# Even slots' middle maxima ahead of their ends, and the 128-column scores ahead of the 384, in a windowed attention with a gated MLP

## The chip, the cores and the metric

One core of one Trainium2 chip runs the whole program. The metric is the device time of one execution in microseconds (us). Engines are named as in the profile: PE (matmul), PEld (its weight loads, which run beside the matmuls), DVE (vector), ACT (scalar), POOL (GpSimd), SP (the queue that issues the transfers).

## The reference

```python
B, S, D = 1, 2048, 512           # H = 32 heads of 16, window W = 256, F = 1792
xn = layernorm(x)
q, k, v = split(xn @ wqkv)
scores = q @ k.T * 16 ** -0.5     # per head; key j is seen by query i where 0 <= i - j < 256
s = (softmax(masked scores) @ v) @ wo
g = silu(gelu(layernorm(xn) @ w1 + b1) @ w2 + b2)
return x + s * g
```

All is float32. The kernel gets products of float32 precision by splitting operands into a high and a low part (two or three matmuls for one).

## The kernel before, in words

The program has three stretches. Up to about 59 us it loads `x`, normalizes it and makes the first projections. From 59 to 391 us it does the attention, with the other projections, and the first of the MLP's matmuls, filled in between. After that come the rest of the MLP, the output projection and the gate. The change touches the second stretch alone.

The attention's work is cut into eight groups of four heads, and each group into 16 slots, one for a block of 128 tokens. One pass of the loop over `u` is a slot pair, called a pair here: an even slot and an odd one, 64 pairs in all. Every instruction goes out in the order in which the code writes it, on each engine (a wrapper keeps the program's order, so nearly all rows of the profile have that wrapper's line, L42, and are told apart by their tiles). On an engine an instruction that waits holds up all that stands behind it.

The tiles in PSUM (eight banks) that matter here:

- `stb`, two banks: scores of a pair, in three parts one after the other. PE fills it, ACT's exponential reads it into a tile `pt`, and only then can PE fill it again. Parts 0 and 1 are two heads each: the first key block against up to 384 queries, and the second key block against its own 128 queries. Part 2 holds the second key block's other 256 queries for all four heads; the last pair of a group has none.
- `xy`, two banks: the *ends* of a row's maximum. For a query block 12 slots ahead (`LEAD`), PE computes the scores with the own key block and the block two before; DVE merges them by the mask (COPY_PREDICATED) and reduces to a maximum, kept in `mt`.
- `zo`, two banks, shared. Columns 0 to 255 of both banks are `mids`, the *middle* of a row's maximum: scores with the key block one before, which DVE reduces into `mt` too. Columns 256 to 511 of the second bank are `otb`, in which PE sums the products of the exponentials with the values (`pv_part`, in the profile `zo<-pt,vt`). ACT copies `otb` to SBUF as `oraw` when a pair's products are done.
- `fb`, two banks: the fills, matmuls of projections or of the MLP, of 512 columns mostly, two at a time in the two halves of the array's rows. A table gives each slot its fills, and `some(parts[...])` issues them.

A score or maximum matmul uses 64 rows of the array, so that those for `a` = 1 and 0 run beside each other.

In a pair PE's order before is: scores part 1, ends, some fills, middle, fills (even slot); scores part 2, fills, middle, fills, ends, fills, scores of the next pair's part 0, and the value products (odd slot). ACT's order is: exponential of part 0, copy `oraw` (of the products just made), exponential of part 1, exponential of part 2, with copies and casts for the projections between. For a group's first block (seven times behind the first pair) there is no middle.

Of the kernel before, what the change touches and what calls it, by code (L numbers as in the profile page):

```python
# [25 lines left out]
LEAD = 12  # L26
# [23 lines left out]
def mixer_kernel(ctx, tc, x, wqk, wv, wo, w1, b1, w2, b2, out):  # L50
# [97 lines left out]
    def run(steps):  # L148
        for step in steps:
            step()  # L150
# [471 lines left out]
    def prob_part(u, part):  # L622

        n, kb = u // 8, 2 * (u % 8)
        if part == 2 and kb == 14:
            return
        slot = slots[n % 2]
        both = stb[0]
        if 16 * n + kb + LEAD >= 16 * NQ and (3 * u + (part + 3) % 3) % 2:
            both = xy  # L630
        pt = pp.tile([P, 2, 512], F32, tag="pt", name=f"pt_{u}_{part}")

        def scores(at_, a, p, k, q, w):
            r = slice(64 * a, 64 * a + 64)
            nc.tensor.matmul(both[:, a, at_: at_ + w], slot[r, 1, p, P * k: P * (k + 1)],
                             slot[r, 0, p, P * q: P * q + w], start=True, stop=True)
        if part < 2:
            w = min(384, S - P * kb)
            for a in (1, 0):
                scores(128, a, part, kb, kb, w)  # L640
            for a in (1, 0):
                scores(0, a, part, kb + 1, kb + 1, 128)
            w += 128
        else:
            w = 512
            for p in range(2):
                for a in (1, 0):
                    scores(256 * p, a, p, kb + 1, kb + 2, 256)
        outs["exp"] = nc.scalar.activation(pt[:, :, 0:w], both[:, :, 0:w], AF.Exp, scale=DH ** -0.5)

        def select(at_, step, pattern, compare, by):
            nc.gpsimd.affine_select(out=at_, in_=at_, pattern=pattern, compare_op=compare, fill=0.0, base=0,
                                    channel_multiplier=by)
        if part < 2:
            own = pt[:, :, 0:256].rearrange("k a (b q) -> k a b q", b=2)
            select(own, 1, [[0, 2], [0, 2], [1, P]], ALU.is_ge, -1)
            if w == 512:
                select(pt[:, :, 384:512], 1, [[0, 2], [-1, P]], ALU.is_gt, 1)
        else:
            last = pt.rearrange("k a (p q) -> k a p q", p=2)[:, :, :, 128:256]  # L660
            select(last, 1, [[0, 2], [0, 2], [-1, P]], ALU.is_gt, 1)
        pts[u, part] = pt

    def pv_part(u):

        n, kb = u // 8, 2 * (u % 8)
        seq = [(kb, lambda j: pts[u, j // 2][:, j % 2, 128:384], 0, 256),
               (kb + 1, lambda j: pts[u, j // 2][:, j % 2, 0:128], 128, 256)]
        if kb:
            seq[:0] = [(kb - 1, lambda j: pts[u - 1, 2][:, j % 2, 256 * (j // 2): 256 * (j // 2 + 1)], 0, 256),  # L670
                       (kb - 2, lambda j: pts[u - 1, j // 2][:, j % 2, 384:512], 0, 128)]
        for i, (k, of, lo, hi) in enumerate(seq):
            for j in range(4):
                nc.tensor.matmul(otb[32 * j: 32 * j + DH + 1, lo: hi], vt[:, k, (4 * n + j) % 16], of(j),
                                 start=(i == 0), stop=(i == len(seq) - 1),
                                 skip_group_check=True, tile_position=(0, 32 * j))
        oraw = sgp.tile([P, 256], F32, tag="or", name=f"oraw_{u}", bufs=2)
        nc.scalar.copy(oraw, otb)
        cols = slice(P * kb, P * (kb + 2))
        at(2 * u + 2, nc.sync.dma_start, oT_d[n, :, :, cols].rearrange("j r t -> (j r) t"), oraw)  # L680
# [256 lines left out]
    def fill_in(t, half):  # L937
        now[:] = t, half
        run(delayed.pop((t, half), ()))
        for fn, args in fills.get((t, half), ()):  # L940
            fn(*args)

    def planned(t):
        for fn, args in plan.get(t, []):
            fn(*args)

    def ended(t):
        for fn, args in ends.get(t, []):
            fn(*args)
# [3 lines left out]
    def own_max(part, m):  # L953
        return part(m // 16, m % 16) if m < end else lambda: None

    def own_rows(m, t):
        if 0 <= m < end and m % 4 == 3:
            max_rows(m // 16, m % 16 // 4, t)

    for t in range(-16, 0):  # L960
        m = t + LEAD
        if t == -5:
            open_slot(1)
            for k in range(4):
                at(-4 + k // 2 * 2, clear_part, k)
        fill_in(t, 0)
        planned(t)
        if 4 <= m < LEAD:
            max_block(0, m)
        fill_in(t, 1)  # L970
        if t == -1:
            early.close()
            stb.append(attn.enter_context(tc.tile_pool(name="ps_s2", bufs=1, space=PSUM)).tile(
                [P, 2, 512], F32, name="stb"))
            prob_part(0, 0)
            fill_in(t, 2)
        if 0 <= m < 4:
            max_block(0, m)
        run(lns.get(t, ()))
        own_rows(m, t)  # L980
        ended(t)
    def parted(todo, *cuts):

        n = sum(fn.__name__ == "unit" for fn, _ in todo)
        at_ = [0, *(-(-n * k // 20) for k in cuts), len(todo)]
        return [todo[a: b] for a, b in zip(at_, at_[1:])]

    def some(todo):
        for fn, args in todo:
            fn(*args)  # L990
    for u in range(end // 2):
        t = 2 * u
        prob_part(u, 1)
        rest = own_max(max_ends, t + LEAD)
        calm[0] = t < end - LEAD
        even, odd = (fills.pop((v, 0), []) for v in (t, t + 1))
        if u % 8:
            parts = parted(even, 5) + parted(odd, 10 if u % 8 == 7 else 5, 15)
        else:
            parts = parted(even + odd, 2, 6, 10, 14)  # L1000
        now[:] = t, 0
        run(delayed.pop((t, 0), ()))
        some(parts[0])
        own_max(max_middle, t + LEAD)
        rest()
        planned(t)
        some(parts[1])
        fill_in(t, 1)
        ended(t)
        t += 1  # L1010
        prob_part(u, 2)
        now[:] = t, 0
        run(delayed.pop((t, 0), ()))
        some(parts[2])
        own_max(max_middle, t + LEAD)
        some(parts[3])
        planned(t)
        fill_in(t, 1)
        own_max(max_ends, t + LEAD)()
        calm[0] = False  # L1020
        own_rows(t + LEAD, t)
        for fn, args in todo_dve:
            fn(*args)
        todo_dve.clear()
        if u % 8:
            some(parts[4])
        if t + 1 < end:
            prob_part(u + 1, 0)
        if u % 8 == 0:
            some(parts[4])  # L1030
        fill_in(t, 2)
        pv_part(u)
        ended(t)
# [29 lines left out]
    for f in range(6, NF, 2):  # L1063
        t = gp.tile([P, 2, 512], F32, tag="ohl", name=f"hr_{f}", bufs=4)
# [200 lines left out]
    for c in range(2):  # L1265
# [30 lines left out]
        for i in range(NF + 1):  # L1296
# [29 lines left out]
            k = i - o_from  # L1326
# [190 lines left out]
```

## Time and profile before

| what | value |
|---|---|
| median of three runs | 712.68 us (711.99 to 713.08) |
| the profiled execution | 711.56 us, its span 709.5 us |
| granted PE clock | 1.00 |
| PE busy | 702.7 us (99%), weight loads 571.9 us (81%) |
| DVE busy | 508.6 us (72%) |
| ACT busy | 407.5 us (57%) |
| POOL busy | 299.3 us (42%) |

The span runs from the first to the last instruction of the profiled execution. A matmul's time in a row includes its way through the array, and, where it waited for its weights, that wait; so the busy share of PE alone doesn't say how full it is, and starts of rows that follow each other say more. A row of the timeline has start, length, engine, line, operation, out<-in, and in brackets how long the engine was idle before it and on what.

### The profile page before, as it was taken

To read this page: it belongs to the slowest core of one execution; us is meant where nothing else is said; L and a number is where in the kernel's file an instruction comes from. 1 tells how busy PE (TensorE), PEld (TensorE's weight loads), DVE (VectorE), ACT (ScalarE), POOL (GpSimd) and SP (SyncE) were. 2 spreads that over 40 slices of the span, in tenths; PEclk is the share of its full clock that TensorE was granted. 3 is DMA by queue.
4 is the path that set the end of the run, shared out by engine and by line. 5 is a ranking of instruction groups with operands and counts; after the bars stand their busy time and mean duration, and the time that the engine had idled before them with its cause. 6 is when DMAs were issued, how large, how long until landed. Compare 5 with 4: busy or idle time off the path is not lost.

```text
span 709.5 us, 17676 instructions
## 1 busy us (share of the span) xinstructions
PE 702.7 (99%) x6912; PEld 571.9 (81%) x6912; DVE 508.6 (72%) x863; ACT 407.5 (57%) x604; POOL 299.3 (42%) x496
## 2 busy tenths in 40 slices
PE   8999999999999999999999999999999999999997
PEld 8999777777778887777777788888888888888886
DVE  7887787887877678788875666347686766766923
ACT  8767777778676667778877554222355545531001
POOL 7344766766676555767877420204203000002002
PEclk9999999999999999999999999999999999999999
DMA  8325466775549967678543747354222312353701
GB/s 307 80 49 123 93 147 156 186 177 133 117 118 272 296 221 231 166 192 206 173 137 114 264 141 264 104 157 154 90 90 89 120 59 90 99 184 125 232 15 60
DMA packets 66274, 106.95 MB, mean 151 GB/s; under 512 B 12624, under 2 KB 21072, under 8 KB 66192
## 3 DMA queue, kind: packets, MB, share of 16 engines
q1 hardware_dynamic: 66192, 105.82, 51.6%
q8 instruction: 55, 0.90, 0.5%
q14 instruction: 27, 0.22, 0.1%
HBM read 54.80 MB, written 33.82 MB: 125 GB/s over the span
## 4 chain that ended last, share of the span: by engine, by line
PE 98%; DMA 1%; DVE 0%; ACT 0%; issue 0%; POOL 0%; SPq 0%; DVEq 0%
PE fb L42 22%; PE acc L42 21%; PE zo L42 15%; PE p L42 9%; PE stb L42 8%; PE s L42 6%; PE h L42 6%; PE xy L42 6%; PE pv L42 2%; DMA x<-in_x_dram 1%; PE tr L42 0%; PE pair_-8_609 L42 0%; PE pair_-5_829 L42 0%; PE pair_-8_608 L42 0%; PE pair_-3_975 L42 0%; PE pair_-3_974 L42 0%
## 5 line engine op out<-in xcount | busy, mean ns | idle before, releaser
L42 ACT ACTIVATE pt<-stb 128x1024 f32<-128x1024 f32 (+1 forms) x176 | 177.6, 1009 | 51.6 <-PE stb L42 44.4
L42 POOL TENSOR_SCALAR_AFFINE_SELECT pt<-pt 128x512 f32<-128x512 f32 (+1 forms) x296 | 163.8, 574 | 72.9 <-ACT pt L42 69.9
L42 PE MATMUL fb<-xnT,wqb 64*128 64x512 f32 (+2 forms) x732 | 118.1, 392 | 0.2
L42 DVE COPY_PREDICATED xy<-upper,xy 128x512 f32<-128x512 int32 x128 | 88.9, 694 | 37.8 <-PE xy L42 35.2
L42 POOL TENSOR_TENSOR xo<-xo,gated 128x512 f32<-128x512 f32 x15 | 20.0, 1330 | 221.7 <-DVE gated L42 220.6
L42 PE MATMUL acc<-w,gh 128*128 128x512 f32 x320 | 98.6, 389 | 0.0
L42 PE MATMUL zo<-pt,vt 128*17 128x128 f32 (+1 forms) x1920 | 90.5, 327 | 0.3
L42 DVE TENSOR_REDUCE mt<-xy 128x4 f32<-128x512 f32 x128 | 88.0, 687 | 2.3
L42 DVE TENSOR_REDUCE mt<-zo 128x4 f32<-128x512 f32 x120 | 82.6, 689 | 6.3 <-PE zo L42 5.8
L42 PE MATMUL stb<-qk 64*128 64x384 f32 (+1 forms) x704 | 77.4, 297 | 0.0
L42 PEld LDWEIGHTS zo<-pt,vt 128*17 128x17 f32 x1920 | 49.1, 97 | 33.6 <-issue 1.3
L42 PEld LDWEIGHTS stb<-qk 64*128 64x128 f32 x704 | 55.4, 185 | 22.8 <-ACT pt L42 13.6
L42 PEld LDWEIGHTS acc<-w,gh 128*128 128x128 f32 x320 | 60.1, 188 | 12.5
L42 PEld LDWEIGHTS fb<-xnT,wqb 64*128 64x128 f32 (+1 forms) x732 | 61.3, 186 | 3.7 <-PE fb L42 1.0
L42 PE MATMUL acc<-w,gl 128*128 128x512 f32 x160 | 62.2, 389 | 0.0
L42 PE MATMUL xy<-qk 64*128 64x256 f32 (+2 forms) x576 | 60.3, 291 | 0.0
L42 PEld LDWEIGHTS xy<-qk 64*128 64x128 f32 x576 | 46.5, 185 | 7.3 <-DVE mt L42 1.2
L42 PE MATMUL p<-xnT 128*128 128x512 f32 x189 | 51.8, 389 | 0.0
L42 PEld LDWEIGHTS zo<-qk 64*128 64x128 f32 x480 | 40.5, 185 | 6.4 <-DVE mt L42 1.7
L42 PE MATMUL s<-wos,ohl 128*128 128x512 f32 (+1 forms) x204 | 44.3, 376 | 0.0
L42 ACT ACTIVATE gated<-acc 128x512 f32<-128x512 f32 x16 | 8.7, 596 | 62.0 <-DVE acc L42 62.0
L42 PE MATMUL fb<-xnT 64*128 64x512 f32 (+1 forms) x240 | 43.7, 403 | 0.5 <-DVE pjr L42 0.5
(205 smaller groups left out, 1214.4 us busy)
## 6 DMA issues: line engine op xcount, KB each, us to landing
qk<-sh SPq DMA_DIRECT2D x128, 128.0 KB
qk<-pjr SPq DMA_DIRECT2D x64, 128.0 KB
oT_d<-oraw SPq DMA_DIRECT2D x64, 128.0 KB
w_d<-in_w_dram SPq DMA_DIRECT2D x14, 512.0 KB
xt_d<-xnT SPq DMA_DIRECT2D x12, 512.0 KB
x<-in_x_dram SPq DMA_DIRECT2D x16, 256.0 KB
w<-w_d SPq DMA_DIRECT2D x16, 256.0 KB
or<-oT_d SPq DMA_DIRECT2D x16, 256.0 KB
```

The lines of the kernel that those rows point to most:

```text
L42: r = issue(*args, **kwargs)
```

## The change

Two things change, both in the attention's pairs. In `prob_part`, part 1's two matmuls of 128 columns come before its two of 384 (part 0 keeps its order). In the loop over `u`, the even slot's middle maxima come directly behind the scores of part 1, and the ends, with DVE's merge and reduction, behind the first fills. The odd slot is as it was.

```diff
         if part < 2:
             w = min(384, S - P * kb)
-            for a in (1, 0):
-                scores(128, a, part, kb, kb, w)
-            for a in (1, 0):
-                scores(0, a, part, kb + 1, kb + 1, 128)
+            for at_, k, wide in ((0, kb + 1, 128), (128, kb, w))[::1 if part else -1]:
+                for a in (1, 0):
+                    scores(at_, a, part, k, k, wide)
             w += 128
...
         prob_part(u, 1)
-        rest = own_max(max_ends, t + LEAD)
+        own_max(max_middle, t + LEAD)
         calm[0] = t < end - LEAD
...
         some(parts[0])
-        own_max(max_middle, t + LEAD)
-        rest()
+        own_max(max_ends, t + LEAD)()
         planned(t)
```

On PE, in an even slot (the pair at 165.7 us), from the scores of part 1 (`stb`) to those of part 2. `xy` are the ends, `zo` from `qk` the middle, `fb` the fills; in brackets stand the engines and transfer queues whose work is waited for. Before:

```order
L42 MATMUL stb<-qk_94 128x384 [waits Activation_49]
L42 MATMUL stb<-qk_94 128x384
L42 MATMUL stb<-qk_94 128x128 x2
L42 MATMUL xy<-qk_764 128x256 [waits DMAHW4_49,DMAHW3_49,DMAHW5_49,DMAHW1_49,DMAHW7_49,DMAHW0_49,DVE_49]
L42 MATMUL xy<-qk_764 128x256 x3
L42 MATMUL fb_112<-xnT,wqb_2503 128x512
L42 MATMUL fb_111<-xnT,wqb_2503 128x512
L42 MATMUL zo<-qk_764 128x128 [waits Activation_49]
L42 MATMUL zo<-qk_764 128x128 x3
L42 MATMUL fb_112<-xnT,wqb_2503 128x512
```

The same place on PE after the change:

```order
L42 MATMUL stb<-qk_94 128x128 [waits Activation_49]
L42 MATMUL stb<-qk_94 128x128
L42 MATMUL stb<-qk_94 128x384 x2
L42 MATMUL zo<-qk_764 128x128 [waits DMAHW5_49,DMAHW3_49,DMAHW7_49,DMAHW1_49,Activation_49]
L42 MATMUL zo<-qk_764 128x128 x3
L42 MATMUL fb_112<-xnT,wqb_2503 128x512
L42 MATMUL fb_111<-xnT,wqb_2503 128x512
L42 MATMUL xy<-qk_764 128x256 [waits DMAHW4_49,DMAHW0_49,DVE_49]
L42 MATMUL xy<-qk_764 128x256 x3
L42 MATMUL fb_112<-xnT,wqb_2503 128x512
```

The middle moved ahead of the ends and of one pair of fills, with its wait for ACT. By the program's counts that wait is for the copy `oraw` of the pair before, which before stood behind the ends and a fill on PE.

ACT's order is the same before and after; here are its rows around the copy for which the next pair's middle waits, with the exponentials (`pt_0`, `pt_1`, `pt_2` are the parts):

```order
L42 ACTIVATE pt_0_3058<-stb 128x1024 [waits PE_49]
L42 COPY oraw_3082<-zo 128x256 [waits DVE_49,DMAHW6_49,PE_49,Activation_49]
L42 ACTIVATE pt_1_3085<-stb 128x1024 [waits PE_49,Pool_49]
L42 ACTIVATE pt_2_3113<-stb 128x1024 [waits PE_49]
L42 COPY pjr_2_3146<-fb_111 128x512 [waits DMAHW1_49,PE_49]
```

Nothing moved on ACT: the copy stands between the exponentials of parts 0 and 1, and waits for PE's products, for DVE, and for the store of an earlier `oraw`.

On DVE, in the same pair, before (`mt` from `zo` is the middle's reduction, `mt` from `xy` that of the ends):

```order
L42 COPY_PREDICATED xy<-upper,xy 128x4x128 [waits PE_49]
L42 TENSOR_REDUCE mt_4_3001<-zo 128x4 [waits PE_49,Activation_49]
L42 TENSOR_REDUCE mt_4_3001<-xy 128x4 [waits DVE_49]
L42 TENSOR_REDUCE mt_4_3001<-zo 128x4 [waits PE_49]
L42 COPY_PREDICATED xy<-upper,xy 128x4x128 [waits DVE_49,PE_49]
```

And after:

```order
L42 TENSOR_REDUCE mt_4_3001<-zo 128x4 [waits PE_49,Activation_49]
L42 COPY_PREDICATED xy<-upper,xy 128x4x128 [waits PE_49]
L42 TENSOR_REDUCE mt_4_3001<-xy 128x4 [waits DVE_49]
L42 TENSOR_REDUCE mt_4_3001<-zo 128x4 [waits PE_49]
L42 COPY_PREDICATED xy<-upper,xy 128x4x128 [waits DVE_49,PE_49]
```

The middle's reduction moved from behind the ends' merge to ahead of it; the odd slot's two behind them stay. POOL's and SP's orders are the same.

## The prediction

> **What bounds the kernel now.** I read the engines' busy shares first, then the row of the attention stretch, then the chain of work there, then the waits, and last the timeline of single slot pairs ("pairs" below; one is a pass of the loop over `u`).
>
> ```profile
> span 709.5 us, 17676 instructions
> 59.00:391.00 332.00, 331.01 (x4868) 258.22 (x4866) 261.28 (x440) 248.31 (x336) 226.26 (x409) 1.00 0.64 172
> by line: PE fb L42 41.0%; PE zo L42 31.6%; PE stb L42 16.5%; PE xy L42 10.4%; DVE pjr L42 0.2%; issue 0.2%; DVE vt L42 0.1%; PE pair_-3_974 L42 0.0%; DVEq L42 0.0%; PE pair_-3_975 L42 0.0%
> PEld stb L42 <- ACT pt L42: 13.6, 63, 0.4
> PEld stb L42 <- issue: 6.5, 31, 0.2
> PEld zo L42 <- DVE mt L42: 1.7, 6, 0.4
> PEld xy L42 <- DVE mt L42: 1.0, 5, 0.2
> ACT oraw L42 <- PE zo L42: 19.3, 41, 0.9
> ```
>
> The second row is the stretch that the change touches, 59 to 391 us: PE busy 331.01 of 332.00 us, DVE 261, ACT 248, clock 1.00. The third is the chain in that stretch: four groups of matmuls hold 99.5% of it. So PE sets the time, and a stall put into its queue comes out at the end unless PE was going to stand there anyway. The waits are small: PE's weight loads for the scores (`stb`) wait 13.6 us for ACT's exponentials and 6.5 us after the value products, some 0.2 us a time, and 2.7 us for DVE's reductions.
>
> **What moves, and the wait that comes with it.** The kinds and numbers of instructions stay, no transfer is moved, and ACT's, POOL's and SP's orders stay. In an even slot PE's four middle-maxima matmuls (128 columns, into `mids`, half of `zo`) now stand right behind the scores; the four of the ends come one fill later. The middle ones wait for ACT, and by the program's counts for one instruction: the copy `oraw<-zo` of the pair before, which empties the other half of a bank that `mids` has a part in. Once in this trace that wait shows by itself:
>
> ```profile
> 108.99 0.37 ACT L42 COPY oraw<-zo 128x256 f32<-128x256 f32 x1 [0.86 <-PE zo L42]
> 109.41 0.30 PEld L42 LDWEIGHTS zo<-qk 64*128 64x128 f32 x4 [0.18 <-ACT oraw L42]
>   PEld zo L42: 0.2, 1
> ```
>
> The copy ends at 109.36 and the weights start at 109.41, 0.05 later. The last row (from the view of that copy, under who waited for it) says that this was felt once, for 0.2 us. In all other pairs the ends and a fill cover it. So the rows say that the wait is live. The Trainium skill (PSUM — Partial Sum Buffer, Terms) speaks against the change at the same place: two engines may not be in one bank and quadrant at once, so the middle maxima could not be let past the copy though their columns differ. If banks could be shared at will, the wait would be worth nothing and the sum below would be a gain of about 1 us; by the rule it is what follows.
>
> **How long PE stands.** Before, the ends' weights go in right behind the scores' matmuls; that row's start is the place the middle maxima take. The copy's end plus 0.05, less that start, is the new stall.
>
> ```profile
> 66.99 0.38 ACT L42 COPY oraw<-zo 128x256 f32<-128x256 f32 x1
> 67.13 0.30 PEld L42 LDWEIGHTS xy<-qk 64*128 64x128 f32 x4
> ...
> 160.51 0.30 PEld L42 LDWEIGHTS stb<-qk 64*128 64x128 f32 x4 [0.22 <-ACT pt L42]
> 160.79 0.30 PEld L42 LDWEIGHTS xy<-qk 64*128 64x128 f32 x4
> 160.81 0.40 ACT L42 COPY oraw<-zo 128x256 f32<-128x256 f32 x1
> ...
> 165.83 0.37 ACT L42 COPY oraw<-zo 128x256 f32<-128x256 f32 x1 [0.43 <-PE zo L42]
> 165.98 0.30 PEld L42 LDWEIGHTS xy<-qk 64*128 64x128 f32 x4
> ...
> 363.71 0.37 ACT L42 COPY oraw<-zo 128x256 f32<-128x256 f32 x1 [0.56 <-PE zo L42]
> 363.81 0.30 PEld L42 LDWEIGHTS xy<-qk 64*128 64x128 f32 x4
> ```
>
> First pair: 66.99 + 0.38 + 0.05 - 67.13 = 0.29. Pair at 165.8: 0.27. Last pair: 0.32. There ACT was free and waited for the value products (41 times in the stretch, by the waits). Where ACT was still at an exponential or a copy, as at 160.81, it is 160.81 + 0.40 + 0.05 - 160.79 = 0.47. Of the 57 pairs behind the first, seven have no middle maxima (a head group's first block). The other 50 run from the first pair above to the last; going through them, 37 are of the first kind (0.25 to 0.38, mean 0.32) and 13 of the second (twelve near 0.47, one 0.60, mean 0.48). 37 x 0.32 + 13 x 0.48 = 18.0 us.
>
> Behind the waiting load on PE stand the fill, the ends, the later fills and the second half's scores; DVE waits for the middle maxima and the ends, ACT for the next scores, POOL for ACT.
>
> **What PE gets back.** Where PE already stood ahead of the second half's scores, the new stall eats that:
>
> ```profile
> 151.77 0.30 PEld L42 LDWEIGHTS stb<-qk 64*128 64x128 f32 x4 [0.35 <-ACT pt L42]
> ...
> 167.38 0.30 PEld L42 LDWEIGHTS stb<-qk 64*128 64x128 f32 x4 [0.17 <-ACT pt L42]
> ```
>
> The usual wait of these weights is 0.17 to 0.19, and at 167.38 the matmuls behind it lose nothing by it (the loads run ahead). At 151.77, in pairs with one fill less, it is 0.35, so 0.18 is real slack. Eight pairs are like that: -8 x 0.2 = -1.6. The bounds are 0 and the 13.6 of the waits' row; I stay near the low end because the chain has no ACT in it.
>
> Second, DVE now reduces the even slot's middle first, about 0.6 us sooner, so the odd slot's middle maxima no longer wait for that. That is bounded by the rows of 1.7 and 1.0 us above, and by 0: I take -1.6, most of the first row, since its cause goes, and none of the second.
>
> **The scores' new order.** With 128 columns ahead of 384 the second weights no longer hide behind a long matmul. Prices:
>
> ```profile
> 405.07 2.72 PE h L42 x12
> 155.68 0.61 PE L42 MATMUL xy<-qk 64*128 64x128 f32 x8
> L42 PE MATMUL zo<-qk 64*128 64x128 f32 x480 | 42.0, 252 | 0.0
> ```
>
> 512 columns take 2.72 / 12 = 0.227, so 128 would stream in 0.057; but eight 128-column matmuls (four concurrent pairs) take 0.61, less the last one's 0.25, over three steps: 0.12 a pair. The first pair therefore holds the 384 back by 0.06, and ACT's exponential starts 0.06 later (bounds 0 and 0.12). PE loses nothing itself: before, the 128 in second place held the next load back as much. In the 50 pairs the later exponential lies under PE's own stall of 0.27 or more; in the seven without middle maxima it comes through: 7 x 0.06 = +0.4.
>
> DVE's order (middle ahead of copy and ends' reduction) is covered: in the pair at 160.5,
>
> ```profile
> 162.55 0.68 DVE L42 TENSOR_REDUCE mt<-xy 128x4 f32<-128x512 f32 x1
> 163.28 0.39 PEld L42 LDWEIGHTS xy<-qk 64*128 64x128 f32 x4
> ```
>
> the even ends are reduced by 163.23. After the change the middle's weights start at 160.81 + 0.40 + 0.05 = 161.26, its matmuls end 0.44 later (the 109.41 case took that), and three DVE steps of 0.60, 0.60 and 0.68 end at 163.63. The odd ends, which need that bank, come at 163.28 + 0.47 = 163.75: just covered. If it were not, each 0.1 us on 50 pairs is 5 us.
>
> **Sum.** 18.0 - 1.6 - 1.6 + 0.4 = +15.2 us. The profiled execution took 711.56 us (span 709.5, and 2.06 around it), which would become 726.8; it lies 1.12 under the median 712.68, so the median becomes **727.9**.
>
> **Rivals.**
> 1. *The score buffer's loop hides the stall* (not slower). One `stb` serves scores, exponential, scores in turn. If that loop and not PE paces a pair, PE's stall fills time that it waits anyway: 13.6 + 6.5 = 20.1 us of waits against 18.0. For it speaks that nearly every score load names ACT. Against it: the chain has no ACT, and the 6.5 us follow the value products, at a place that the stall does not reach. It decides if most of the 0.17 us waits prove real. Then between -2.1 and, with the 13.6 alone, +4.4: 711 to 717.
> 2. *ACT's copy or DVE slips further.* The copy now stands on PE's path, with all that it waits for itself (a store of the buffer two pairs back, DVE's reduction of the same banks: 0.86 us of idle at 108.99). If that costs another 0.1 to 0.2 a pair, 5 to 10 us more: 733 to 738. Against it: 41 of the copies start as soon as the products are done.
> 3. *The wait is met already* (the change does only what its words say). It decides if the copy ends 0.27 to 0.47 sooner; then -1.6 + 0.4: 711.5. Against it: the row at 109.41, and no instruction ahead of the copy goes away.
> 4. *PE's clock drops.* Its granted clock is 1.00 in the stretch's row with some hundred waits of about 0.2 in it. At half clock for a tenth of the stretch, 33 us more: 761. The Trainium skill (TensorE: Matmul & The Clock Gate, A second HAM failure mode) reports such a drop from frequent small gaps between groups of matmuls; no run here shows one.
>
> **How the numbers follow.** Forecast 0.80, first rival 0.08, second 0.08, third 0.03, fourth 0.01. The forecast's own range is 722 to 732: low with three times the slack and all 2.7 us of DVE's waits back (18.0 - 5 - 2.7 = 10.3) , high with nothing given back (18.4). For 8 in 10 I give 719.5 to 732.5, reaching some way to the first rival. About 0.2% (1.4 us) is what a measurement can tell: faster 0.04 (the third rival and part of the first), same 0.04 (the first), slower 0.92.
>
> **What would show it.** Right: weight loads of `zo` waiting for ACT's `oraw` some 50 times, about 0.3 to 0.5 us each, ACT and DVE idle longer per pair, pairs of 5.5 us where they took 5.2, the time outside 59 to 391 us unchanged, and no `zo` load waiting for DVE's `mt`. Wrong: those waits present but the waits of `stb` for ACT gone in exchange (first rival), or no such waits (third). A stretch longer by over 20 us with DVE as the releaser would be the second.

## The result, and the profile after

| kernel | median, us | ratio to before | 95% interval |
|---|---|---|---|
| before | 712.34 | 1 | |
| changed | 730.06 | 1.0257 | 1.0245 to 1.0269 |

The change costs 17.7 us by the medians, 2.5%; the forecast was 727.9, 15.6 above this median, with a range of 719.5 to 732.5. Below, effects are ratios times 712.3 us, so that runs on other chips can be set beside each other: the change is +18.3.

First the span, the attention stretch and what lies behind it, in the changed kernel (busy time of PE, PEld, DVE, ACT and POOL, then clock, share of the transfer engines, GB/s):

```profile
span 728.0 us, 17683 instructions
59.00:409.00 350.00, 343.50 (x4860) 258.03 (x4860) 264.47 (x440) 248.22 (x335) 225.18 (x408) 1.00 0.61 163
409.00:728.00 319.00, 315.33 (x1438) 260.75 (x1436) 198.77 (x325) 114.45 (x188) 42.10 (x32) 1.00 0.40 130
```

and the last stretch of the kernel before:

```profile
391.00:709.50 318.50, 314.77 (x1432) 260.29 (x1428) 199.61 (x325) 113.95 (x187) 42.72 (x31) 1.00 0.40 130
```

The stretch of 332 us has become one of about 350; what follows it is as long as before, and the clock is 1.00 as before. PE was idle for 1.0 us there and is now for 6.5 by the rows. Its busy time grew by another 12.5 (343.50 for 331.01) for the same work: most of the stall lies inside the rows of matmuls that wait for their weights. The waits of PE's loads in that stretch:

```profile
PEld zo L42 <- ACT oraw L42: 16.9, 50, 0.6
PEld xy L42 <- DVE mt L42: 10.8, 37, 0.9
PEld stb L42 <- ACT pt L42: 7.1, 32, 0.3
PEld stb L42 <- issue: 6.5, 31, 0.2
PEld zo L42 <- DVE mt L42: 0.2, 1, 0.2
DVE mt L42 <- PE zo L42: 44.4, 49, 1.8
```

The first row is the forecast's wait: 50 times, 16.9 us, where before it was once and 0.2. The third row is what PE got back ahead of the scores (13.6 before), the fifth the odd middle's wait for DVE (1.7 before). The second row is the one that was not forecast: the loads of the ends wait 10.8 us for DVE, where it was 1.0. The last row is DVE's own: it waits 49 times for the middle's matmuls, 44.4 us, where it was 15 times and 5.8. Here is the pair that stood at 165.8 us before, in the timeline after the change:

```profile
171.96 0.30 PEld L42 LDWEIGHTS stb<-qk 64*128 64x128 f32 x4 [0.21 <-issue]
172.10 0.37 ACT L42 COPY oraw<-zo 128x256 f32<-128x256 f32 x1 [0.43 <-PE zo L42]
172.53 0.30 PEld L42 LDWEIGHTS zo<-qk 64*128 64x128 f32 x4 [0.26 <-ACT oraw L42]
173.07 0.69 DVE L42 TENSOR_REDUCE mt<-zo 128x4 f32<-128x512 f32 x1 [0.46 <-PE zo L42]
173.68 0.69 DVE L42 COPY_PREDICATED xy<-upper,xy 128x512 f32<-128x512 int32 x1
174.40 0.69 DVE L42 TENSOR_REDUCE mt<-xy 128x4 f32<-128x512 f32 x1
175.15 0.30 PEld L42 LDWEIGHTS xy<-qk 64*128 64x128 f32 x4 [0.16 <-DVE mt L42]
```

The copy ends at 172.47, the middle's weights start at 172.53 after 0.26 us of idle (forecast for this pair: 0.27). DVE can't begin before 173.07, does its three steps, and ends at 175.09; the odd ends' weights start 0.06 later, at 175.15, after 0.16 us of idle. By these rows the one copy holds PE up twice: directly, and then through DVE. The chain of work, in the next pair, names the copy:

```profile
176.13 1.47 PE zo L42 x32
177.60 0.03 ACTq L42
177.63 0.04 issue
177.67 0.38 ACT oraw L42
178.05 0.04 issue
178.09 0.44 PE zo L42 x4
```

Value products, copy, middle: between two matmuls of PE stands ACT's copy, where the chain before had PE alone. In the whole stretch the copy has 3.5% of the chain and DVE's steps (`mt` and `xy`) 6.8%.

### The profile page after: what moved, and what is told of

The parts are those of the page before. It is cut to its first block, busy times and chain, and to the rows that moved or that the text cites. A ratio compares the mean times of both kernels' runs of the same rounds, so it can differ in the third digit from the quotient of the medians.

```text
span 728.0 us, 17683 instructions
## 1 busy us (share of the span) xinstructions
PE 715.2 (98%) x6912; PEld 571.7 (79%) x6912; DVE 510.9 (70%) x863; ACT 408.0 (56%) x604; POOL 297.5 (41%) x496
## 4 chain that ended last, share of the span: by engine, by line
PE 89%; DVE 4%; ACT 4%; issue 1%; DMA 1%; POOL 0%; SPq 0%; ACTq 0%; DVEq 0%
PE acc L42 21%; PE fb L42 19%; PE zo L42 14%; PE p L42 9%; PE s L42 6%; PE h L42 6%; PE xy L42 5%; PE stb L42 5%; DVE mt L42 2%; ACT oraw L42 2%; PE pv L42 2%; DVE xy L42 1%; ACT pt L42 1%; ACT pjr L42 1%; DMA w_d<-in_w_dram 1%
## 5 line engine op out<-in xcount | busy, mean ns | idle before, releaser
L42 DVE TENSOR_REDUCE mt<-zo 128x4 f32<-128x512 f32 x120 | 82.5, 688 | 47.3 <-PE zo L42 44.4
L42 PE MATMUL stb<-qk 64*128 64x384 f32 (+2 forms) x704 | 79.2, 303 | 0.0
L42 PEld LDWEIGHTS stb<-qk 64*128 64x128 f32 x704 | 58.3, 185 | 18.9 <-ACT pt L42 7.1
L42 PEld LDWEIGHTS zo<-qk 64*128 64x128 f32 x480 | 39.8, 185 | 19.6 <-ACT oraw L42 16.9
L42 PE MATMUL zo<-qk 64*128 64x128 f32 x480 | 45.5, 267 | 4.6 <-ACT oraw L42 2.8
```

The lines of the kernel that those rows point to most:

```text
L42: r = issue(*args, **kwargs)
```

## The experiments

**The two halves of the change, each alone.** Scores' order alone (in the kernel before):

```diff
-            for a in (1, 0):
-                scores(128, a, part, kb, kb, w)
-            for a in (1, 0):
-                scores(0, a, part, kb + 1, kb + 1, 128)
+            for at_, k, wide in ((0, kb + 1, 128), (128, kb, w))[::1 if part else -1]:
+                for a in (1, 0):
+                    scores(at_, a, part, k, k, wide)
```

> Only the scores' order is changed: 128 columns ahead of 384 in part 1, the maxima as before. Theory (the order costs by itself once nothing covers it): the exponential of part 1 starts 0.06 us later, and in the some 49 pairs in which the second half's scores follow it closely the pair gets 0.05 longer: +2.5 us, 714.8 (713.5 to 716). Rival (PE loses nothing by it, what the prediction's term said for pairs with a cover): no change, 712.3.

Measured: 712.46, ratio 1.0006 (0.9993 to 1.0020), that is +0.4 us (-0.5 to +1.4). The theory's +2.5 is out; the rival holds within the interval. Maxima moved alone (the changed kernel with the old order of the scores):

```diff
-            for at_, k, wide in ((0, kb + 1, 128), (128, kb, w))[::1 if part else -1]:
-                for a in (1, 0):
-                    scores(at_, a, part, k, k, wide)
+            for a in (1, 0):
+                scores(128, a, part, kb, kb, w)
+            for a in (1, 0):
+                scores(0, a, part, kb + 1, kb + 1, 128)
```

> Only the maxima are moved, the scores' order is as before. Theory (PE stands for ACT's copy, and the later exponential lies under that stall): all of the change but 0.4 us is here: 729.6 (729 to 730.1). Rival (the scores' order is a good part of the loss, some 0.05 us a pair everywhere): 727.5.

Measured: 730.03, ratio 1.0241 (1.0222 to 1.0259), +17.2 us, the wait for the copy 17.0 us in 50 loads. All of the loss, but for what the intervals can't tell, is in the moved maxima.

**The wait taken away.** ACT's copy keeps its place in the order and its columns, but reads a constant; PE then has nothing to wait for there. The copy takes 0.40 us in place of 0.37, and it no longer waits for the value products, so it also comes earlier on ACT. The edit is the same in both kernels, so that the kernel before is the control:

```diff
-        nc.scalar.copy(oraw, otb)
+        nc.scalar.copy(oraw, vt[:, 0, 0, DH: DH + 1].to_broadcast([P, 256]))
```

> The changed kernel, but ACT's copy reads a constant from SBUF in place of the value products (these are computed and not delivered), so that nothing on PE waits for it; its time on ACT stays. Theory (the wait for the copy is the cause, DVE's lateness follows from it): the 18.0 us stall and the 4.9 us of the odd ends behind DVE go, the scores' order shows its 2.5: about 710 (708 to 713). Rival (DVE's new order delays the odd ends by itself): some 5 us stay, 715 to 718. Rival (the wait is not the cause): 728 and over.

> The control for that: the kernel before with the same copy from SBUF in place of the value products (not delivered). All theories: the wait is covered there but for 0.2 us and a few late copies, so 711.5 (710 to 712.3). If it were much below, taking the wait away would be worth something in either order, and the other run would have to be read against this one.

Measured: the changed kernel 713.33, ratio 1.0011 (1.0001 to 1.0022); the kernel before 711.95, ratio 0.9991 (0.9978 to 1.0004). With the wait gone, 1.0257 falls to 1.0011: 17.5 of 18.3 us hang on it, or 16.9 if the control's gain of 0.6 is taken off. The waits of PE's loads, in the changed kernel with the constant copy:

```profile
PEld stb L42 <- ACT pt L42: 17.6, 68, 1.4
PEld stb L42 <- ACT oraw L42: 6.1, 29, 0.2
PEld xy L42 <- DVE mt L42: 3.8, 14, 0.5
```

No `zo` load waits for the copy any more, and the ends' wait for DVE falls from 10.8 to 3.8 by itself: DVE was late because the middle was. (The second row stands where "issue" stood, with 6.5 us: the copy is there only the last event that came before.) The time came out 3 us above the theory's 710, just outside its range of 708 to 713. The theory had taken off 18.0 + 4.9 = 22.9 us, more than the 17.7 that the change had cost: it counted on what PE gets back to stay, a gain from DVE's order among it, and that gain wasn't there. What of the last 1.4 us between this kernel and its control is whose, the next run asked: the same, with the scores' order as before (the edit of the second run and the one above together).

> The maxima moved, the scores' order as before, and ACT's copy from SBUF (the value products not delivered), so that PE waits for no copy. Theory (without the wait the new order of the maxima is about neutral, and the 1.4 us between the two kernels with the copy from SBUF are the scores' order): 711.5 to 712.3, level with the kernel before. Rival (the 1.4 us come from DVE's order): 713 to 714.

Measured: 712.13, ratio 0.9998 (0.9989 to 1.0006). Without the wait the new order of the maxima is worth nothing either way, though the ends still wait for DVE a little:

```profile
PEld stb L42 <- ACT pt L42: 14.3, 65, 0.4
PEld xy L42 <- DVE mt L42: 5.6, 23, 0.5
```

That leaves about 1 us (1.0011 less 0.9998) for the scores' order where no stall covers it; the three comparisons that hold it (this one, +0.4 alone, 18.3 against 17.2) agree in sign, and none is by itself clear of its interval.

**A shorter copy.** Half of the columns, and so half of the value products left out:

```diff
-        nc.scalar.copy(oraw, otb)
+        nc.scalar.copy(oraw[:, 0:128], otb[:, 0:128])
+        nc.gpsimd.memset(oraw[:, 128:256], 1.0)
```

> The changed kernel with ACT's copy of the value products cut to half of its columns (the other half of the products is left out, POOL fills in ones). Theory (the copy's end sets the stall): the exponentials of 1024 and 768 columns take 1.03 and 0.81 us, so 128 columns less are 0.11 us less; 50 pairs x 0.11 = 5.5 us, and up to 2.5 more where DVE follows: 722 to 725. Rival (DVE's order or the scores' order, not the copy): 729 to 730.

Measured: 727.25, ratio 1.0193 (1.0170 to 1.0216), +13.7 us, 4.6 less than the full copy, outside the theory's 722 to 725 and short of its rival's 729 to 730. The rows say why: all copies (least, median and longest in ns), one pair in the timeline, and the wait in the stretch.

```profile
L42 ACT COPY oraw<-zo x64: 266/266/297, 67.5 to 410.8; 128x128 f32<-128x128 f32 x64
```

```profile
171.35 0.30 PEld L42 LDWEIGHTS stb<-qk 64*128 64x128 f32 x4 [0.21 <-issue]
171.53 0.27 ACT L42 COPY oraw<-zo 128x128 f32<-128x128 f32 x1 [0.47 <-POOL mh L42]
171.85 0.30 PEld L42 LDWEIGHTS zo<-qk 64*128 64x128 f32 x4 [0.20 <-ACT oraw L42]
```

```profile
PEld zo L42 <- ACT oraw L42: 13.8, 49, 0.6
```

The copy is 0.11 us shorter (0.266 for 0.372), but it waits for POOL besides, because of the added memset, and starts 0.18 behind the scores' weights instead of 0.14 (172.10 - 171.96). In this pair 0.06 us is left (0.20 of idle for 0.26), and over all 3.1 us less wait (13.8 for 16.9). The dose comes out clean only where ACT is still at another instruction when the products are done, so that it starts 0.30 behind the scores' weights in both kernels. Here is the middle's load in such a pair, with the full copy and with the half:

```profile
167.01 0.30 PEld L42 LDWEIGHTS zo<-qk 64*128 64x128 f32 x4 [0.46 <-ACT oraw L42]
166.40 0.30 PEld L42 LDWEIGHTS zo<-qk 64*128 64x128 f32 x4 [0.35 <-ACT oraw L42]
```

There the wait falls by the whole 0.11, and it does so in the twelve pairs of this kind. The stall followed the copy's end, not its length.

**A cover for the wait, and DVE out of the way.** Three kernels. The middle behind the first fill:

```diff
         prob_part(u, 1)
-        own_max(max_middle, t + LEAD)
...
         some(parts[0])
+        own_max(max_middle, t + LEAD)
         own_max(max_ends, t + LEAD)()
```

> The changed kernel with the even middle behind the first fill, directly ahead of the ends. The fill (0.227) covers part of the wait: 0.32 - 0.23 in 37 pairs and 0.48 - 0.23 in 13 are left, 6.6 us in place of 18.0. Theory A (only PE's stall counts): 730.1 - 11.4 = 718.7. Theory B (the copy's end also sets when DVE can begin, and DVE's chain of three then holds the odd ends): the ends come 0.2 sooner on PE and wait that much longer for DVE, so that most of it is lost again, 724 to 728.

DVE's merge left out in the even slots, with the maxima as changed:

```diff
-        nc.vector.copy_predicated(own, mask, ends_of[:, :, :, 0])
+        if merge:                      # the even slots' call passes False
+            nc.vector.copy_predicated(own, mask, ends_of[:, :, :, 0])
```

> The changed kernel with DVE's merge (COPY_PREDICATED) left out in the even slots, so that the ends' maximum is that of the own block alone. DVE is some 0.6 us sooner done with the even slot. Theory (the odd ends wait for DVE, 4.9 us over the stretch, on top of the stall): 725 (724 to 726). Rival (the stall for the copy is all, the odd ends' waits lie beside it): 729.5 to 730.

Both edits together:

> Both at once: the even middle behind the first fill, and DVE's merge left out in the even slots. Theory (two waits in a row, PE for ACT's copy, then the odd ends for DVE, and each alone keeps most of the loss): with DVE out of the way the fill's cover of 0.227 comes through, 6.6 us of stall are left, less the 3 of slack and of DVE's waits that come back: 716 to 719. Rival (the fill covers little whatever DVE does): 722 to 724, what leaving out the merge gave alone.

And the merge left out in the kernel before, as the control:

> The control for the two runs without the merge: the kernel before with DVE's merge left out in the even slots (the ends' maximum is that of the own block alone). Theory (DVE holds nothing up there; PE's loads wait 2.7 us for it in all): 710.5 to 712.3, so that the 6.3 us which leaving it out gave the changed kernel are DVE's lateness behind the copy. Rival (a lighter DVE is worth as much in any order): 706 to 707.

| | with the merge | without it |
|---|---|---|
| middle directly behind the scores | +18.3 (1.0257) | +12.0 (1.0168, 1.0149 to 1.0187) |
| middle behind the first fill | +15.5 (1.0218, 1.0200 to 1.0237) | +3.1 (1.0044, 1.0028 to 1.0059) |
| kernel before | 0 | -1.4 (0.9980, 0.9967 to 0.9992) |

(Medians of the four new kernels, line by line: 725.22, 728.81, 715.12 and 710.55 us.) The fill should cover 11.4 us of PE's stall. With DVE's merge in place it gives 2.8; with the merge out it gives 8.9. That is theory B: two waits in a row. Its size was at the edge: the median of 728.81 is above the 724 to 728 that B gave, and on that chip the kernel before took 713.27; by the ratio it is 727.8. With both edits the time, 715.1, came out under the 716 to 719 expected, so the two together cover more than was thought. The rows of the kernel with the fill first, merge in, then merge out:

```profile
PEld xy L42 <- DVE mt L42: 20.5, 45, 0.9
PEld stb L42 <- ACT pt L42: 10.5, 46, 0.4
PEld zo L42 <- ACT oraw L42: 5.1, 27, 0.5
```

```profile
PEld stb L42 <- ACT pt L42: 11.2, 49, 0.4
PEld zo L42 <- ACT oraw L42: 5.1, 27, 0.5
```

In both the wait for the copy falls from 16.9 to 5.1. In the first, the ends' wait for DVE rises from 10.8 to 20.5: PE comes sooner to a bank that DVE can't give back sooner. In the second that row is gone, and so is most of the loss. Leaving out the merge is worth 1.4 us in the kernel before and 6.3 in the changed one, so DVE's lateness behind the copy costs 6.3 - 1.4 = 4.9 us of the 18.3 (about 3 to 7 by the three intervals). None of the kernels here that do the whole computation is faster than the one before.

## Why the prediction was right, point by point

**PE sets the time, and a stall in its queue comes out.** Right: the stretch grew by 18 us, the rest by 0.5, and with the wait taken away the time is back to 713.

**The wait is live, on this copy, 50 times, 18.0 us.** Right: 50 loads, 16.9 us of load idle, and the pair at 172 came out at 0.26 for 0.27. The forecast's formula (the copy's end plus 0.05) is what the rows show: 172.47, then 172.53. The row at 109.41 of the trace before, one wait of 0.18 us in the whole trace, told all of it. The trace fits what the Trainium skill says (PSUM — Partial Sum Buffer, Terms), that two engines may not be in one bank and quadrant at once: the program's wait held the middle maxima, although their columns are others than the copy's. What the chip would do without that wait no run here shows.

**What PE gets back, 1.6 of slack and 1.6 from DVE.** Right in direction: the waits of `stb` for ACT fell by 6.5, those of `zo` for DVE by 1.5. The fall of 6.5 is also half of the first rival's sign, but it did not save the time. How much of it was real slack was not measured by itself.

**The scores' order, +0.4.** Not told apart: +0.4 (-0.5 to +1.4) alone, about 1 without a cover. My second thought, the 2.5 us of the first experiment's theory, was wrong; the prediction's smaller term was nearer.

**DVE's order is covered ("just covered").** Wrong, and this is the step that failed: the odd ends wait for DVE 37 times, worth 4.9 us. The term stood at 0, with a margin of 0.12 us less 0.05. Two things in it were mis-sized. I let the first reduction begin 0.49 us behind the middle's weights (the 0.44 of the matmuls and 0.05 more, which the working doesn't name but its 163.63 holds); it is 0.54 (172.53 to 173.07). And I gave the second step 0.60 us; it is 0.72 (173.68 to 174.40). Before, the order was merge, middle, ends, so that another instruction stood between the merge and the reduction that reads its result:

```profile
166.53 0.70 DVE L42 COPY_PREDICATED xy<-upper,xy 128x512 f32<-128x512 int32 x1 [0.17 <-PE xy L42]
167.13 0.69 DVE L42 TENSOR_REDUCE mt<-zo 128x4 f32<-128x512 f32 x1
167.74 0.68 DVE L42 TENSOR_REDUCE mt<-xy 128x4 f32<-128x512 f32 x1
```

Now that reduction stands right behind the merge and waits for its result. The odd slots of the trace before had this order all along, with the longer step:

```profile
163.92 0.70 DVE L42 COPY_PREDICATED xy<-upper,xy 128x512 f32<-128x512 int32 x1
164.65 0.69 DVE L42 TENSOR_REDUCE mt<-xy 128x4 f32<-128x512 f32 x1
```

It is 0.73 from start to start there, so the trace before already held the figure. 0.05 + 0.12 us more than planned is past the margin of 0.07. The longer step costs only together with the late start: the kernel with the moved maxima and the constant copy has the same order on DVE and is level with the kernel before (0.9998). So the second rival (0.08) was in part true beside the forecast: its mechanism came, at 4.9 us, just under the 5 to 10 it was priced at. The sum came out 3 us low for this, and the rest of it was a little high: 18.3 - 4.9 = 13.4 against 15.2. That the two errors went against each other is luck. With the rest as summed, 4.9 us more would have made 732.8, just outside the range.

**The other rivals.** The score buffer's loop did not hide the stall (+18 and not -2 to +4), the wait was not met already, and the clock stayed at 1.00 with some 80 more waits for the copy and for DVE in the stretch.

## What to carry to other kernels

Before an instruction is moved ahead, look at what it waits for at its old place, also where that wait has cost nothing: one short row that names the releaser is enough, and its end plus the 0.05 us to the next start gives the price at the new place. Then follow the same release into the next engine: here a cover for PE's stall alone gave 2.8 of 11.4 us, because DVE began late from the same cause, and the two could only be seen apart by easing both. And count a new order of the same work anew: on DVE here, a reduction right behind the merge whose result it reads started 0.12 us later than one that had another instruction's work between.

## What the runs showed that I had not expected

On DVE, two independent instructions of 0.69 us start 0.60 to 0.61 apart (166.53, 167.13 and 167.74 before; 173.07 and 173.68 after), and where the second reads the first's result, 0.72 to 0.73. In the changed kernel that holds for every one of the 117 merges that their own reduction follows directly.

And with one more wait on ACT's copy (the one for POOL, with the memset) its start came 0.04 us further behind the scores in the pair shown, and 0.08 in 22 others, so that a copy shortened by 0.11 ended only 0.03 to 0.06 sooner. Whether the wait itself takes that time was not tested.
